# A fast attention, then an expert mixture: two more periods of short products in place of plain half layers

## The chip, the core and the metric
The kernel runs on one core of a Trainium2 chip: TensorE (matmuls; its weight loads are shown apart), VectorE (DVE), ScalarE (ACT), GpSimd (POOL), and SyncE (SP), which issues nearly all DMAs. The metric is the time of one execution in microseconds; before the change it is 1458.92 us, the median of 3 runs (1458.7 to 1458.94). The profile shows one execution.

## The reference
A gated linear attention over 4 batches, 8 heads, 768 steps of 48 wide heads, and behind it a dense mixture of 8 experts, with gates balanced by 8 rounds of row and column division:
```python
for t in range(S):
    state = f[:, :, t, :, None] * state + np.einsum('bhd,bhe->bhde', k[:, :, t], v[:, :, t])
    y[:, :, t] = einsum('bhd,bhde->bhe', q[:, :, t], state)
...
logits = x @ w_gate; P = exp(logits - logits.max())
for _ in range(8):
    P /= P.sum(1, keepdims=True) + 1e-09
    P /= P.sum(0, keepdims=True) + 1e-09
    P *= N / E
for e in range(E):                      # x: 3072 x 384, w1: 384 x 1024, w2: 1024 x 384
    out += P[:, e:e + 1] * (maximum(x @ w1[e], 0) @ w2[e])
```

## The kernel before
**Numbers.** Every product of 32-bit values is made of three 16-bit products (high by high, high by low, low by high). So each value is split: ScalarE writes the high part, VectorE or GpSimd the low part (the difference). `hh` and `hl` are the two parts of a hidden layer, `xh`/`xl` of the tokens, `sh`/`sl` of the attention's state.

**Attention.** 24 items of 128 tokens, each a chain of some 30 steps over all engines (`item`, L713): sigmoid of the gates, two scans (L732, L751), products (`aps`), the state (`st`, L814) and its parts (`sh` L821, `sl` L829), the output products (`yps`, the last eight of which read `sl`), the tokens' parts (L847, L850). A new item begins every 8 steps (STEPS), so three or four are under way. Each engine's order is fixed as the program is written (`pin`, `mm`): an engine that waits for one instruction holds up all behind it.

**Filler.** While the items run, TensorE works on experts 0 and 1 in the plain way. After each attention step `fill` (L955) takes as many units of this work as the table FILL says for that step; a unit is one matmul of 384 columns or three of 128. The work stands in `raw_pairs` (L941): for the first three half batches (u below TILED) it goes by tiles of 128 tokens (`moe_tile`, L444: a first layer `hps` in groups of four blocks, 36 matmuls of 128 columns each, ReLU into `hh` and `hl`, then a second layer `yps` of 384 columns, copied to `yr` and written to memory); for later ones by half batches of 384 tokens (`moe`, L400). A tile may only begin when its tokens are there. Then the gates are balanced, a chain of small steps between which LEAD units of the same filler are laid.

**Periods.** The rest goes by a scheme that makes block products of sums of blocks, with fewer products: ORDER (L96) lists the periods (expert, half of its hidden width, batch), 50 of them, each 15 slots: 90 matmuls of 256 columns for the first layer (banks `kb_A` to `kb_F`) and 126 of 192 columns for the second layer of the period before (`paired`, L1348: `kyps`, `kxps`). EVENTS says in which slot ScalarE, VectorE and GpSimd do what with the banks (`kr`, `kf`, `kgh`, `kgl`, `kal`); weights are prepared by `prepare_w1` and `prepare_w2` in the slots of W1AT, W2AT and their relatives. HALVED (L95) lists the batches of which expert 1's second half is made in periods at the end of ORDER; `plain` (L397) says how many of the 8 blocks of the hidden width the plain way does. It is used in `moe` alone. After the last period ENDING (L94) orders what is left: a '.' is one slot's events, a digit n takes block n two stages further.

Of the kernel before, what the change touches and what calls it, by code (L numbers as in the profile page):

```python
# [78 lines left out]
END = 27  # L79
W1AT = (0, 1, 2, 3, 5, 9, 10, 11, 12, 21, 23, 25, 26)  # L80
W1AT0 = (16, 18, 19, 19, 22, 23, 23, 27, 27, 33, 35, 40, 41)
W2AT = (4, 22, 25, 25, 27, 29, 30, 35, 38)
W2AT0 = (0, 1, 1, 3, 3, 5, 5, 5, 7)
W2AT1 = (3, 8, 10, 12, 13, 13, 14, 14, 19)
W2AT3 = (0, 3, 6, 13, 15, 18, 20, 21, 26)
READDAT = (9, 14)
CHECKAT = (1, 5)
# [3 lines left out]
ENDY = (None, None, 'B', 'D')  # L91
CONVAT = (3, 6, 7, 9, 11)
LAST_EVENTS = {18: (('gs', 'C', 1, 1), ('gs', 'C', 1, 2), ('hl', 'C', 1)), 19: (('gs', 'C', 1, 3), ('gf', 'F', 2), ('gh', 1, 0), ('gh', 1, 1))}
ENDING = '.0.1.01.1..12.1.22..23.23.34343444'  # L94
HALVED = (2, 3)  # L95
ORDER = [(e, m, b) for e in range(2, NE) for m in range(2) for b in range(B)] + [(1, 1, b) for b in HALVED]  # L96
PAIRED = (0, 1, 2)
BY_POOL = (1,)
# [9 lines left out]
TS = CT * C  # L108
ONES = CT * NP * D * 4
LEADS = 23  # L110
FILL = ((0, 11.7), (1, 10.3), (2, 0), (3, 0), (5, 2), (6, 0), (7, 6), (8, 6), (9, 0), (10, 6), (12, 5.3), (15, 5.3), (17, 5.3), (23, 8.7), (30, 8.7), (43, 8.0), (195, 7))
LEAD = 6.9
FIRSTAT = ((0,), (0,), (0, 4), (0, 7), (1, 9), (5, 10))
SECONDAT = ((16, 17), (18, 20), (17, 18), (17, 21), (20, 21), (20, 22), (24, 24), (24, 25))
# [169 lines left out]
def fast(ctx, tc, qkf, vbd, wg, w1, w2, out, flag):  # L284
# [37 lines left out]
    wctx, wctx0, wctx2, actx, pctx = (ExitStack() for _ in range(5))  # L322
    wp2 = wctx2.enter_context(tc.tile_pool(name="wp2", bufs=4, side="right"))
    wp1 = wctx.enter_context(tc.tile_pool(name="wp1", bufs=4, side="right"))
    wp0 = wctx0.enter_context(tc.tile_pool(name="wp0", bufs=8, side="right"))
    ap = actx.enter_context(tc.tile_pool(name="ap", bufs=2, side="right"))
    dp = ctx.enter_context(tc.tile_pool(name="dp", bufs=1, space=DRAM))
    psm = ctx.enter_context(tc.tile_pool(name="psm", bufs=2, space=PSUM))
# [113 lines left out]
    tiles, put_off, owed = [0], [False], []  # L442

    def moe_tile(e, u, t):  # L444
        w1s, w2s = ws[e]
        if (u, t) not in ready:
            raise RuntimeError("an expert is ahead of its tokens")
        xh, xl = xof(u)
        ts = slice(t * 128, t * 128 + 128)
        h = []  # L450
        for g in range(2):
            ps = bank([128, 4, 128], f"hps_{e}_{u}_{t}_{g}")
            n = 0
            for q, x in ((0, xh), (0, xl), (1, xh)):
                for f in range(4 * g, 4 * g + 4):
                    a = w1s[f // 2][q]
                    fs = slice((f % 2) * 128, (f % 2) * 128 + 128)
                    for k in range(KT):
                        mm(out=ps[:, f % 4, :], lhsT=a[:, k, fs], rhs=x[:, k, ts], start=(n == 0), stop=(q == 1 and k == KT - 1), skip_group_check=True)
                        n += 1  # L460
                        if n < 36:
                            yield 1 / 3
            i = tiles[0] % FT
            tiles[0] += 1
            th, tl = (hp.tile([128, 2, 256], F16, name=f"h{q}_{e}_{u}_{t}_{g}", tag=f"k{q}{i // 6}{i % 6 // 3}{i % 3}").rearrange("p c t -> p (c t)") for q in "hl")
# [12 lines left out]
        ps = bank([128, DM], f"yps_{e}_{u}_{t}")
        n = 0
        for f in range(FT):  # L480
            if len(owed) > 1 - f // 4:
                raise RuntimeError("a low part is owed")
            wh, wl = w2s[f // 2]
            hh, hl = (v[:, f % 4, :] for v in h[f // 4])
            for a, b in ((hh, wh), (hh, wl), (hl, wh)):
                mm(out=ps, lhsT=a, rhs=b[:, f % 2, :], start=(n == 0), stop=(n == 3 * FT - 1))
                n += 1
                if n < 3 * FT:
                    yield 1
# [449 lines left out]
    ws = [([None] * 4, [None] * 4) for e in range(NE)]  # L939

    def raw_pairs(pairs):  # L941
        for e in range(2):
            for t in range(TT):
                yield from moe_tile(e, 0, t)
        for u in range(1, TILED):
            for t in range(TT):
                for e in range(2):
                    yield from moe_tile(e, u, t)
        for e, u in pairs:
            if u >= TILED:  # L950
                yield from moe(e, u, ws[e])
# [138 lines left out]
        return (lambda: xq), lambda: sums(b), [x32[:, k].rearrange("p u t -> p (u t)") for k in range(KT)]  # L1090

    first = [load(0, 1 + n // 4, n % 4) for n in range(8)]
    second = [load(1, 1 + n // 4, n % 4) for n in range(8)]
    wgen = gate_weights()
    it = early_item(0)
    go(it)
# [22 lines left out]
    live, g = [it, nxt], 0  # L1119
    for n in range(2, 8):  # L1120
        at_steps(first[n], *FIRSTAT[n - 2])
    for n in range(8):
        at_steps(second[n], 4 + n, *SECONDAT[n])
    begin = {LEADS + STEPS * (i - 3): i for i in range(3, NT)}
    begin_tail = max(begin) + 17
# [339 lines left out]
    def at_all(n, slots, gen):  # L1465
        for slot in slots:
            at_slots(n + slot // PRODUCTS, (slot % PRODUCTS,), gen)

    for n, (e, m, b) in enumerate(ORDER):
        part = n % 4  # L1470
        if n - part + 4 < PERIODS and part in (0, 2):
            e2, m2, _ = ORDER[n - part + 4]
            gen = prepare_w1(e2, 2 * m2 + part // 2)
            at_all(n, W1AT if n else W1AT0, gen)
        if n == 0:
            at_all(0, W2AT0, prepare_w2(e, 2 * m))
            at_all(0, W2AT1, prepare_w2(e, 2 * m + 1))
        if n - part + 4 < PERIODS and (n in (1, 3) if n < 4 else part in (0, 2)):
            e2, m2, _ = ORDER[n - part + 4]
            at_all(n, W2AT if n != 3 else W2AT3, prepare_w2(e2, 2 * m2 + part // 2))  # L1480
        if n >= FIRST_READD:
            at_slots(n, READDAT, again)
        if n >= 5 and part in (1, 3):
            for s in CHECKAT:
                plan.setdefault((n, s), []).append(lambda: next(checks, None))
        if n >= 6 and part in (0, 2):
            at_slots(n, MAXAT, maxima)
        if n >= PERIODS - 2:
            at_slots(n, VERDICTAT[n - PERIODS], judged)
# [200 lines left out]
```

## Time and profile before
| | before |
|---|---|
| median of 3 runs | 1458.92 us |
| the profiled execution | 1458.97 us, its span 1457.2 us |
| TensorE busy | 1435.4 us (99%), 16188 matmuls |
| VectorE, ScalarE, GpSimd busy | 1241.6, 1112.2, 1092.3 us |
| attention items 3 to 23 (first to last mask product) | 78.6 to 346.3 us |
| the periods | from about 442 us |

Busy time of TensorE is modelled for its ends and its matmuls overlap; whether it is dense is read from the distance of the starts. Busy time of the others is measured.

### The profile page before, as it was taken

Reading aid. Unit: us, or ns where it says so; the run is one execution under the profiler, and the core shown is the slowest. Engines: PE = TensorE matmul, PEld = TensorE weight load, DVE = VectorE, ACT = ScalarE, POOL = GpSimd, SP = SyncE. Lnnn points to the kernel's source line nnn. Section 1 sums busy time; section 2 is a strip of 40 time slices with the busy share of each in tenths; the row PEclk is TensorE's granted clock in tenths of the full one; section 3 lists DMA queues with packets and bytes.
Section 4 is the critical chain, followed back from the end, with each engine's and each line's share of the span. In section 5 each row is a group of like instructions: output and inputs, shape, how many; then the busy total and the mean of one; then the engine's idle time right before and its main releaser. Section 6 shows DMA issues by size and latency. Waiting matters only on the chain.

```text
span 1457.2 us, 40795 instructions
## 1 busy us (share of the span) xinstructions
PE 1435.4 (99%) x16188; PEld 1267.0 (87%) x16188; DVE 1241.6 (85%) x2540; ACT 1112.2 (76%) x2492; POOL 1092.3 (75%) x1288
## 2 busy tenths in 40 slices
PE   7999999999999999999999999999999999999997
PEld 5788886666568899999999999999999999999997
DVE  8868878877868998888899898888888889888886
ACT  7767778875547778888888888888777787778874
POOL 3244665675625769999999999999888888888874
PEclk9999999999999999999999999999999999999999
DMA  9245544541111011222211111111000000000201
GB/s 265 84 113 132 120 110 126 124 120 47 65 49 35 24 40 47 56 62 61 61 55 58 49 50 45 41 51 49 23 23 24 23 23 23 13 15 20 77 13 69
DMA packets 82955, 90.54 MB, mean 62 GB/s; under 512 B 50017, under 2 KB 69601, under 8 KB 82754
## 3 DMA queue, kind: packets, MB, share of 16 engines
q1 hardware_dynamic: 82322, 87.25, 21.6%
q8 instruction: 128, 2.10, 0.6%
q14 instruction: 73, 0.60, 0.1%
q10 hardware_dynamic: 432, 0.59, 0.1%
HBM read 64.03 MB, written 14.16 MB: 54 GB/s over the span
## 4 chain that ended last, share of the span: by engine, by line
PE 73%; DVE 3%; ACT 1%; POOL 0%; issue 0%; ACTq 0%; POOLq 0%; DVEq 0%
PE kyps L312 29%; PE kb_A L312 9%; PE kb_B L312 8%; PE kb_D L312 6%; PE kxps L312 5%; PE kb_C L312 4%; PE yps L312 4%; PE hps L312 3%; PE kb_E L312 2%; PE kb_F L312 2%; DVE k1l L1228 0%; DVE kf L1538 0%; DVE kl L1569 0%; POOL k1s L1216 0%; DVE acc L1387 0%
## 5 line engine op out<-in xcount | busy, mean ns | idle before, releaser
L312 PEld LDWEIGHTS <-k1h 128*128 128x128 f16 x3000 | 282.5, 98 | 21.4 <-issue 1.1
L312 PE MATMUL kyps<-k2h,kgl 128*128 128x192 f16 x1188 | 292.3, 246 | 0.6 <-POOL kgl L1564 0.6
L312 PE MATMUL kyps<-k2h,kgh 128*128 128x192 f16 x1188 | 292.3, 246 | 0.1
L312 PE MATMUL kyps<-k2l,kgh 128*128 128x192 f16 x1188 | 292.2, 246 | 0.0
L312 PEld LDWEIGHTS <-kgh 128*128 128x128 f16 x2400 | 220.9, 98 | 7.2 <-issue 0.5
L1564 POOL TENSOR_TENSOR kgl<-kf,kgh 128x512 f16<-128x512 f32 x148 | 198.4, 1341 | 2.1 <-ACT kgh L1561 2.1
L1387 DVE SCALAR_TENSOR_TENSOR yy<-kyps,pes,part 128x192 f32<-128x192 f32 x270 | 111.5, 413 | 92.5 <-PE kyps L312 82.3
L1564 POOL TENSOR_TENSOR kgl<-kr,kgh 128x512 f16<-128x512 f32 x148 | 175.4, 1185 | 9.1 <-PE kyps L312 7.7
L1430 POOL TENSOR_TENSOR acc<-acc,yy 128x384 f32<-128x384 f32 x135 | 134.9, 1000 | 58.4 <-DVE yy L1387 58.4
L312 PEld LDWEIGHTS <-k1l 128*128 128x128 f16 x1500 | 146.8, 98 | 16.9
L312 PEld LDWEIGHTS <-kh 128*128 128x128 f16 x1200 | 112.6, 98 | 7.9 <-issue 1.3
L312 PEld LDWEIGHTS <-kgl 128*128 128x128 f16 x1200 | 117.4, 98 | 0.9 <-POOL kgl L1564 0.8
L312 PEld LDWEIGHTS <-w1h 128*128 128x128 f16 x1248 | 87.9, 98 | 27.1 <-issue 2.1
L312 PE MATMUL yps<-w2h,hl 128*128 128x384 f16 x336 | 110.1, 328 | 1.0 <-DVE hl L470 0.9
L312 PE MATMUL yps<-w2l,hh 128*128 128x384 f16 x336 | 110.0, 328 | 0.6 <-DVE w2l L385 0.6
L312 PE MATMUL yps<-w2h,hh 128*128 128x384 f16 x336 | 110.1, 328 | 0.2 <-ACT hh L420 0.2
L1515 ACT ACTIVATE cp<-kb_A 128x512 f32<-128x512 f32 x150 | 89.8, 599 | 17.5 <-DVE kb_A L1517 15.9
L1541 POOL TENSOR_TENSOR kr<-kr 128x256 f32<-128x256 f32 x100 | 75.6, 756 | 33.5 <-DVE xbl L1029 26.4
L312 PEld LDWEIGHTS <-hh 128*128 128x128 f16 x672 | 65.1, 99 | 37.2 <-issue 1.0
L1384 ACT ACTIVATE kyps<-kyps 128x192 f32<-128x192 f32 x148 | 47.7, 322 | 65.2 <-PE kyps L312 65.1
L1561 ACT ACTIVATE kgh<-kf 128x512 f16<-128x512 f32 x150 | 94.9, 633 | 1.7 <-DVE kf L1538 1.6
L1561 ACT ACTIVATE kgh<-kr 128x512 f16<-128x512 f32 x150 | 94.3, 629 | 0.6 <-DVE kr L1538 0.6
(323 smaller groups left out, 5383.6 us busy)
## 6 DMA issues: line engine op xcount, KB each, us to landing
q<-in_qkf_dram SPq DMA_DIRECT2D x23, 672.0 KB, 5.0
k1r<-in_w_dram SPq DMA_DIRECT2D x26, 384.0 KB, 3.0
k2r<-in_w_dram SPq DMA_DIRECT2D x26, 384.0 KB, 3.0
ys<-yr SPq DMA_DIRECT2D x48, 192.0 KB, 2.4
yb<-ys SPq DMA_DIRECT2D x48, 192.0 KB, 2.4
vr<-in_vbd_dram SPq DMA_DIRECT2D x24, 192.0 KB, 2.5
out_dram<-acc SPq DMA_DIRECT2D x21, 192.0 KB, 1.9
w1r<-in_w_dram SPq DMA_DIRECT2D x8, 384.0 KB, 9.4
```

The costliest lines, as they stand in the source:

```text
L312: ins = (nc.tensor.transpose if transpose else nc.tensor.matmul)(**kw)
L1384: pin(nc.scalar.activation(out=out, in_=in_, func=AF.Copy, **kw))
L1387: pin(nc.vector.scalar_tensor_tensor(out=y, in0=ps, scalar=p, in1=z, op0=ALU.mult, op1=ALU.add))
L1430: pin(nc.gpsimd.tensor_tensor(out=y, in0=y, in1=z.rearrange("p s d -> p (s d)"), op=ALU.add))
L1515: pin(nc.scalar.activation(out=fresh(ev[2]), in_=bk, func=AF.Copy))
L1541: pin((nc.gpsimd if ev[2] == 'P' else nc.vector).tensor_tensor(out=r[:, 0], in0=r[:, 1], in1=r[:, 0], op=ALU.subtract))
L1561: pin(nc.scalar.activation(out=hs['g', t][0][i], in_=hs['f' if i else 'r', t], func=AF.Copy))
L1564: pin((nc.vector if tag == str(PERIODS - 1) and ev[1] else nc.gpsimd).tensor_tensor(out=hs['g', t][1][i], in0=hs['f' if i else 'r', t], in ...
```

## The change
HALVED takes batches 0 and 1 too, so ORDER has 52 periods and expert 1 does half of its hidden width in the plain way for all tokens; `moe_tile` learns `plain`. Four loads of expert 1's weights go, and its pool holds four tiles. `moe_tile` yields 0 between its layers, and `raw_pairs` uses that to run the first layer of one tile ahead of the second layer of another. FILL gives fewer units for each step from 23 on (5.2 then 6.6, before 8.7 then 8.0). Two tables of preparation steps for the first periods and ENDING are different.
```diff
-W1AT0 = (16, 18, 19, 19, 22, 23, 23, 27, 27, 33, 35, 40, 41)
+W1AT0 = (16, 18, 19, 19, 22, 23, 23, 25, 26, 26, 29, 37, 40)
+W2ATB = (4, 12, 20, 20, 21, 22, 22, 35, 38)
-ENDING = '.0.1.01.1..12.1.22..23.23.34343444'
-HALVED = (2, 3)
+ENDING = '.0.1.01.11..2.1.22..23.23.34343444'
+HALVED = (0, 1, 2, 3)
-FILL = (... (17, 5.3), (23, 8.7), (30, 8.7), (43, 8.0), (195, 7))
+FILL = (... (17, 5.3), (23, 5.2), (43, 6.6), (107, 6.6), (195, 6.5))
-    wp0 = wctx0.enter_context(tc.tile_pool(name="wp0", bufs=8, side="right"))
+    wp0 = wctx0.enter_context(tc.tile_pool(name="wp0", bufs=4, side="right"))
...
-        for g in range(2):
+        fts = plain(e, u)
+        for g in range(fts // 4):
...
             yield 1 / 3
+        yield 0
         ps = bank([128, DM], f"yps_{e}_{u}_{t}")
         n = 0
-        for f in range(FT):
-            if len(owed) > 1 - f // 4:
+        for f in range(fts):
+            if len(owed) > fts // 4 - 1 - f // 4:
...
+        pending = []
+
+        def hidden(e, u, t):
+            gen = moe_tile(e, u, t)
+            for cost in gen:
+                if not cost:
+                    break
+                yield cost
+            pending.append(gen)
+
+        def rest(most):
+            while len(pending) > most:
+                yield from pending.pop(0)
+
         for e in range(2):
             for t in range(TT):
-                yield from moe_tile(e, 0, t)
+                yield from hidden(e, 0, t)
+                yield from rest(1 if plain(e, 0) < FT and t < TT - 1 else 0)
         for u in range(1, TILED):
             for t in range(TT):
                 for e in range(2):
-                    yield from moe_tile(e, u, t)
+                    yield from hidden(e, u, t)
+                    yield from rest(1 if e == 0 and plain(1, u) < FT else 0)
...
-    second = [load(1, 1 + n // 4, n % 4) for n in range(8)]
+    second = {n: load(1, 1 + n // 4, n % 4) for n in (0, 1, 4, 5)}
...
-            at_all(n, W2AT if n != 3 else W2AT3, prepare_w2(e2, 2 * m2 + part // 2))
+            at_all(n, {1: W2ATB, 3: W2AT3}.get(n, W2AT), prepare_w2(e2, 2 * m2 + part // 2))
```
The order on ScalarE in the attention, where the tile of expert 0 and then that of expert 1 go through (`hh_e_u_t_g` is group g of a tile's hidden layer, `yr_e_u_t` its result; `ft`, `tds`, `vhc`, `vh`, `xh`, `kb`, `vl`, `qh`, `ah`, `sh` belong to items). Before:
```order
L467 ACTIVATE hh_0_1_0_1_1885<-hps_0_1_0_1_1842 128x512
L725 ACTIVATE ft0_125<-q3_6_1778 112x8x63
L727 ACTIVATE tds_154<-q3_6_1778 112x8
L742 ACTIVATE vhc_6_1915<-vr_6_1780 128x384
L744 ACTIVATE vh0_136<-vr_6_1780 64x8x48 x2
L491 ACTIVATE yr_0_1_0_1990<-yps_0_1_0_1889 128x384
L847 ACTIVATE xh0_313<-yps_4_1928 96x3x128
L847 ACTIVATE xh0_313<-yps_4_1928 32x128 x3
L761 ACTIVATE kb0_124<-q3_6_1778 48x8x64 x2
L766 ACTIVATE vl0_140<-vlc_6_1916 64x8x48 x2
L467 ACTIVATE hh_1_1_0_0_2100<-hps_1_1_0_0_1993 128x512
```
The same place now:
```order
L745 ACTIVATE vhc_6_1733<-vr_6_1599 128x384
L747 ACTIVATE vh0_136<-vr_6_1599 64x8x48 x2
L469 ACTIVATE hh_1_1_0_0_1819<-hps_1_1_0_0_1717 128x512
L850 ACTIVATE xh0_313<-yps_4_1758 96x3x128
L850 ACTIVATE xh0_313<-yps_4_1758 32x128 x3
L764 ACTIVATE kb0_124<-q3_6_1597 48x8x64 x2
L769 ACTIVATE vl0_140<-vlc_6_1734 64x8x48 x2
L775 ACTIVATE qh_6_1896<-q3_6_1597 112x512
L494 ACTIVATE yr_0_1_0_1923<-yps_0_1_0_1823 128x384
L816 ACTIVATE ah_5_1928<-am_5_1912 128x512
L824 ACTIVATE sh1_146<-st_5_1807 48x8x48 x2
L494 ACTIVATE yr_1_1_0_1947<-yps_1_1_0_1926 128x384
```
Before, a tile's result `yr_0_1_0` stands ahead of the next tile's `hh_1_1_0_0`. Now expert 1's only group stands ahead of both results, and the pieces of the items stand closer to each other, with less filler between them.

The order on VectorE in the ending; blocks of period 48 (before) and 50 (now) are finished while the hidden layers of the last period, 49 and 51, are made. Before:
```order
L1569 SCALAR_TENSOR_TENSOR kl_49_1_26320<-kb_49_C_26529,kh_49_1_26319 128x512
L1538 SCALAR_TENSOR_TENSOR kf_49_1_26747<-kb_49_C_26529,kf_49_1_26747 128x256
L1550 SCALAR_TENSOR_TENSOR kal_49_2_26720<-kb_49_F_26590,kah_49_2_26719 128x256
L1387 SCALAR_TENSOR_TENSOR acc2_9129<-kxps_48_2_26696,pes_119,acc2_9129 128x192
L1387 SCALAR_TENSOR_TENSOR yy_48_2_26698<-kyps_48_2_26695,pes_119,part_48_2_26697 128x192
L1564 TENSOR_TENSOR kgl0_49_1_26761<-kr_49_1_26647,kgh0_49_1_26759 128x512
L1564 TENSOR_TENSOR kgl1_49_1_26762<-kf_49_1_26747,kgh1_49_1_26760 128x512
L1387 SCALAR_TENSOR_TENSOR acc2_9129<-kyps_48_2_26695,pes_119,acc2_9129 128x192
L1387 SCALAR_TENSOR_TENSOR yy_48_2_26698<-kyps_48_2_26695,pes_119,part_48_2_26697 128x192
```
The same place now:
```order
L1588 SCALAR_TENSOR_TENSOR kl_51_1_26423<-kb_51_C_26636,kh_51_1_26422 128x512
L1406 SCALAR_TENSOR_TENSOR acc2_8536<-kxps_50_2_26803,pes_119,acc2_8536 128x192
L1406 SCALAR_TENSOR_TENSOR yy_50_2_26805<-kyps_50_2_26802,pes_119,part_50_2_26804 128x192
L1557 SCALAR_TENSOR_TENSOR kf_51_1_26854<-kb_51_C_26636,kf_51_1_26854 128x256
L1569 SCALAR_TENSOR_TENSOR kal_51_2_26827<-kb_51_F_26697,kah_51_2_26826 128x256
L1583 TENSOR_TENSOR kgl0_51_1_26876<-kr_51_1_26754,kgh0_51_1_26874 128x512
L1583 TENSOR_TENSOR kgl1_51_1_26877<-kf_51_1_26854,kgh1_51_1_26875 128x512
L1406 SCALAR_TENSOR_TENSOR acc2_8536<-kyps_50_2_26802,pes_119,acc2_8536 128x192
L1406 SCALAR_TENSOR_TENSOR yy_50_2_26805<-kyps_50_2_26802,pes_119,part_50_2_26804 128x192
```
The additions into `acc2` and `yy` of the third block of the last period but one have gone ahead of the last `kf` and of `kal`.

## Rows read from the trace of the kernel before

**Rows 1.** the page, busy time of each engine in the whole execution
```profile
PE 1435.4 (99%) x16188; PEld 1267.0 (87%) x16188; DVE 1241.6 (85%) x2540; ACT 1112.2 (76%) x2492; POOL 1092.3 (75%) x1288
```

**Rows 2.** windows: length, busy us (instructions) PE, PEld, DVE, ACT, POOL, clock, DMA
```profile
36.70:78.60 41.90, 39.40 (x562) 31.32 (x561) 33.80 (x55) 31.79 (x61) 14.43 (x14) 1.00 0.33 90
78.60:346.30 267.70, 266.13 (x3901) 202.19 (x3899) 214.18 (x412) 201.96 (x435) 154.68 (x167) 1.00 0.47 116
228.30:281.00 52.70, 52.39 (x661) 36.02 (x659) 45.78 (x88) 42.45 (x92) 28.14 (x31) 1.00 0.52 126
...
442.00:500.00 58.00, 56.60 (x580) 51.86 (x579) 51.47 (x109) 45.83 (x105) 40.10 (x53) 1.00 0.09 29
600.00:1400.00 800.00, 799.86 (x8542) 759.24 (x8540) 706.21 (x1479) 645.36 (x1485) 711.80 (x830) 1.00 0.13 40
```

**Rows 3.** timeline of TensorE: start, length, engine, line, operation, count
```profile
119.81 0.33 PE L312 MATMUL yps<-w2l,hh 128*128 128x384 f16 x1
...
122.57 0.83 PE L312 MATMUL hps<-xh,w1h 128*128 128x128 f16 x12
123.24 0.83 PE L312 MATMUL hps<-xl,w1h 128*128 128x128 f16 x12
```

**Rows 4.** waits of TensorE from 33 us on: us in total, times, longest
```profile
PE kyps L312 <- DVE yy L1387: 1.2, 1, 1.2
PE yps L312 <- DVE hl L470: 0.9, 2, 0.7
PE kyps L312 <- POOL kgl L1564: 0.6, 1, 0.6
...
PE yps L312 <- DVE sl L829: 0.3, 1, 0.3
```

**Rows 5.** VectorE by shape, attention stretch: busy us, mean ns, idle before
```profile
L829 DVE SCALAR_TENSOR_TENSOR sl<-st,sh 48x384 f16<-48x384 f32 x34 | 29.0, 853 | 4.1 <-ACT sh L821 3.7
...
L421 DVE SCALAR_TENSOR_TENSOR hl<-hps,hh 128x384 f16<-128x384 f32 x36 | 19.7, 550 | 18.1 <-ACT hh L420 17.6
L470 DVE SCALAR_TENSOR_TENSOR hl<-hps,hh 128x512 f16<-128x512 f32 x27 | 18.4, 683 | 22.6 <-ACT hh L467 22.6
```

**Rows 6.** ScalarE, groups by shape in the attention stretch
```profile
L420 ACT ACTIVATE hh<-hps 128x384 f16<-128x384 f32 x36 | 17.5, 485 | 5.1 <-PE hps L312 4.6
...
L467 ACT ACTIVATE hh<-hps 128x512 f16<-128x512 f32 x26 | 15.5, 596 | 9.5 <-PE hps L312 9.2
...
L491 ACT ACTIVATE yr<-yps 128x384 f32<-128x384 f32 x14 | 6.8, 489 | 14.4 <-PE yps L312 9.0 <-issue 5.2 <-ACT sh L821 0.3
```

**Rows 7.** timeline of VectorE ahead of item 7's last products
```profile
137.85 0.69 DVE L470 SCALAR_TENSOR_TENSOR hl<-hps,hh 128x512 f16<-128x512 f32 x1 [1.05 <-ACT hh L467]
138.46 1.11 DVE L829 SCALAR_TENSOR_TENSOR sl<-st,sh 48x384 f16<-48x384 f32 x2
```

**Rows 8.** timeline of TensorE, matmuls that read sl in items 7 and 16
```profile
141.11 0.40 PE L312 MATMUL yps<-qh,sl 112*128 112x64 f16 x8
...
261.52 0.41 PE L312 MATMUL yps<-qh,sl 112*128 112x64 f16 x8 [0.31 <-DVE sl L829]
```

**Rows 9.** timeline of the ending, three engines around TensorE's wait
```profile
1438.46 0.41 DVE L1538 SCALAR_TENSOR_TENSOR kf<-kb_C,kf 128x256 f32<-128x256 f32 x1
...
1438.90 0.63 ACT L1561 ACTIVATE kgh<-kf 128x512 f16<-128x512 f32 x1 [0.63 <-DVE kf L1538]
...
1439.44 0.41 DVE L1387 SCALAR_TENSOR_TENSOR yy<-kyps,pes,part 128x192 f32<-128x192 f32 x1
...
1439.90 0.24 PE L312 MATMUL kyps<-k2h,kh 128*128 128x192 f16 x1 [1.16 <-DVE yy L1387]
```

**Rows 10.** timeline of item 5, GpSimd and VectorE side by side
```profile
109.61 1.16 POOL L822 TENSOR_TENSOR al<-am,ah 128x512 f16<-128x512 f32 x1 [2.08 <-ACT ah L813]
...
110.52 2.10 DVE L829 SCALAR_TENSOR_TENSOR sl<-st,sh 48x384 f16<-48x384 f32 x2 [0.65 <-ACT sh L821]
...
110.72 1.48 POOL L775 TENSOR_TENSOR ql<-q,qh 112x512 f16<-112x512 f32 x1
```

More of the change, by code (lines that the diff above doesn't have):

```diff
@@ L110 @@
 LEADS = 23
-FILL = ((0, 11.7), (1, 10.3), (2, 0), (3, 0), (5, 2), (6, 0), (7, 6), (8, 6), (9, 0), (10, 6), (12, 5.3), (15, 5.3), (17, 5.3), (23, 8.7), (30, 8.7), (43, 8.0), (195, 7))
+FILL = ((0, 11.7), (1, 10.3), (2, 0), (3, 0), (5, 2), (6, 0), (7, 6), (8, 6), (9, 0), (10, 6), (12, 5.3), (15, 5.3), (17, 5.3), (23, 5.2), (43, 6.6), (107, 6.6), (195, 6.5))
 LEAD = 6.9
@@ L485, in moe_tile @@
             for a, b in ((hh, wh), (hh, wl), (hl, wh)):
-                mm(out=ps, lhsT=a, rhs=b[:, f % 2, :], start=(n == 0), stop=(n == 3 * FT - 1))
+                mm(out=ps, lhsT=a, rhs=b[:, f % 2, :], start=(n == 0), stop=(n == 3 * fts - 1))
                 n += 1
-                if n < 3 * FT:
+                if n < 3 * fts:
                     yield 1
@@ L1121, in fast @@
         at_steps(first[n], *FIRSTAT[n - 2])
-    for n in range(8):
+    for n in second:
         at_steps(second[n], 4 + n, *SECONDAT[n])
```

## The prediction
> **What bounds the kernel now.** I read the page first: TensorE is busy for 99% of the span, VectorE for 85% [rows 1]. Busy there is not full speed, so I took the windows by stage next. In the attention stretch (78.6 to 346.3 us, items 3 to 23) TensorE is busy for 266.13 of 267.70 us, VectorE for 214.18 (80%), ScalarE for 201.96 (75%), GpSimd for 154.68 (58%); in the periods (600 to 1400 us) TensorE idles for 0.14 of 800 us [rows 2]. The timeline then says whether busy means dense. From 119.81 to 122.57 us lie 17 matmuls of 384 columns, one after the other: 162.4 ns each. Twelve of 128 columns take 0.67 us: 55.8 ns each [rows 3]. So TensorE sets the pace, and fewer matmuls mean less time as long as nobody makes it wait. The waits of TensorE come last: beyond the start they are few, 1.2 us for one addition in the ending, 0.9 us for low parts of the hidden layer, 0.6 for a low part made by GpSimd, 0.3 for the low part of the state [rows 4]. What the reader should keep from this: TensorE is the bound everywhere, but in the attention stretch VectorE and ScalarE are only 20 to 25% away from it.
>
> **What the matmuls give.** HALVED takes expert 1's second half for batches 0 and 1 out of the plain layers. By the order of instructions 324 matmuls of 128 columns go (nine tiles, 36 each), 36 first-layer and 144 second-layer matmuls of 384 columns: 324 x 55.8 ns + 180 x 162.4 ns = 18.1 + 29.2 = 47.3 us [rows 3]. Two periods come: 216 matmuls each, and 8542 matmuls in the 800 us of periods make 93.65 ns a matmul, 20.23 us a period [rows 2], 40.5 us for two. Net -6.85 us. All of what a period has on the other engines lies inside this 20.23 us, where they are hidden already; the two new ones use weights that are prepared anyway, so no preparation is added. Four weight loads with their conversions leave the start.
>
> **Where it is taken from.** By the order, between the first matmul of item 3 and that of item 23 there are 267 fewer matmuls of 128 columns, 116 fewer second-layer and 36 fewer first-layer ones: 14.9 + 18.8 + 5.8 = 39.5 us. Another 6.9 us lie before item 3, 0.8 behind item 23. So nearly all of it comes out of the stretch in which the other engines are fullest; the attention work itself stays. Were TensorE dense throughout, the stretch would last 267.7 - 39.5 = 228.2 us.
>
> VectorE sheds only the low parts of the dropped hidden tiles there: 7 of 683 ns and 4 of 550 ns [rows 5], 7.0 us, so it needs 207.2 of 228.2 us: 91%, from 80%. ScalarE sheds 7 x 596 + 4 x 485 ns and gains one copy of a result (about 485 ns, as the same engine takes for the same width) [rows 6]: 196.3 us, 86%. GpSimd sheds nothing: 68%.
>
> Does TensorE wait for that? The tightest handoff is the low part of the state, sl, which the last eight matmuls of an item read. In item 7 sl ends at 138.46 + 1.11 = 139.57 us and TensorE comes to it at 141.11: 1.54 us spare; in item 16 nothing is spare and TensorE waits 0.31 us [rows 7, 8]. The 21 items read in this way lie between these two or a little above (to 3.2 us), the middle one at 1.8. Six attention steps lie between an item's first products and these matmuls, and each loses 1.4 units (8.0 to 6.6) of 162.4 ns: 1.36 us in all. If sl were made just as long after those products as now, the spare time of a middle item shrinks to 0.4 us, and the four tightest items (spare 0.06 to 1.25) lose 1.3, 0.5, 0.3 and 0.1 us: 2.2 us. Against that, VectorE stands idle before hl because it waits for ScalarE, 22.6 + 17.6 us in the stretch [rows 5], and 1.05 us of it before sl in item 7 [rows 7]; a faster TensorE lets these waits shrink. For it, the load of 91% with hardly a lull. I take 3.0 us of new waits, near the count by items; the lower end is -0.3 (the present sl wait gone as well), the upper end is under the rivals.
>
> **The order of tiles.** In the first tiled token tiles the second layer of expert 0 now stands behind the first layer of expert 1. That gives the low part hl the time of 36 matmuls of 128 columns (2.0 us) before it is read, where TensorE waited 0.9 us in two places [rows 4]. ScalarE and VectorE have the same instructions. The gain is at most 0.9. In the other direction the steps 23 to 42 lose 3.5 units each, 0.57 us a step, which brings items 3 and 4 closer to what they need; from 36.7 to 78.6 us TensorE loses 6.9 of 41.9 us and VectorE, busy for 33.80 [rows 2], loses two low parts and four weight conversions, some 5 us, so its share stays near 81%. I let these cancel: 0, with -0.9 and +3 as ends.
>
> **The period tables.** W1AT0 and W2ATB issue preparation steps of the first periods up to ten slots earlier, on SP, ScalarE, VectorE and GpSimd. TensorE idles for 1.40 us from 442 to 500 us [rows 2], 0.6 of it for GpSimd's kgl [rows 4]. The steps could clear that or double it: 0, with -1.4 and +1.4 as ends.
>
> **The ending.** TensorE's order there is unchanged. On VectorE two additions (acc, yy) go ahead of kf and kal. TensorE stands 1.16 us until yy, which starts at 1439.44; kf starts at 1438.46, three places earlier, so a place is worth 0.33 us and yy comes 0.65 us earlier [rows 9]. Behind kf, which is now two places late, waits ScalarE's kgh [rows 9], and behind that its copies for the next block; this takes back some of it. -0.5, between -0.65 and +0.3.
>
> **The sum.** -6.85 + 3.0 + 0 + 0 - 0.5 = -4.35. The profiled execution took 1458.97 us (span 1457.2 and 1.8 around it), 0.05 above the median of the runs: 1454.6 us.
>
> **The rivals.**
> 1. Everything arrives. Spare time holds because VectorE's idle time before hl is what goes. For it: VectorE runs nearly without a pause where it is late and TensorE is not held up (0.3 us in 21 items). Against: item 16, and three more with 1.3 us or less to spare. -6.85 - 0.65 - 0.9 = -8.4: 1450.6 us.
> 2. No change. TensorE waits a third of a microsecond for sl or hl in each of the 21 items, 7.0 us in place of 3.0: 1458.6 us. For it: the order in which VectorE works is fixed, so each late result delays what is queued behind it.
> 3. VectorE becomes the bound of the attention stretch, and it is slower. From 228.3 to 281.0 us, the fullest stretch of this length, it is busy for 45.78 of 52.70 us, 87% [rows 2]; if in-order waits between it, ScalarE and GpSimd allow no more over the whole stretch, its 207.2 us last 238.2, 10.0 more than TensorE needs: -6.85 - 0.5 + 10.0 = +2.65. Collisions with GpSimd add: in item 5 GpSimd's al and ql run from 109.61 to 112.20 us, and the two sl instructions beside them take 2.10 us [rows 10], where a pair alone takes 1.11 [rows 7]. 34 long ones average 853 ns against 555: 10 us in the stretch [rows 5]. With GpSimd at 68% instead of 58% that becomes 11.7, VectorE's need 208.9, and its stretch 240.1: the time would be 1458.97 - 7.35 + 11.9 = 1463.5 us. It decides from 207.2 / (228.2 + 7.35) = 88%: below this share of VectorE the change loses. Against: that 87% was seen while TensorE set the pace, and part of the rest was waiting for TensorE's own products.
>
> On these collisions the Trainium skill ("SBUF — State Buffer", Who interferes with whom) says that a VectorE instruction with two SBUF inputs and a GpSimd instruction that reads SBUF exclude each other for their whole length. The trace agrees: the second sl of that item runs to just behind the end of ql. By the rule each meeting costs whole instructions, so rival 3 deserves more than the mean load alone would give it.
>
> **How the numbers follow.** Chances: forecast 0.42 (own range 1452.4 to 1457.0), rival 1 0.25, rival 2 0.15, rival 3 0.18. About 0.2%, 2.9 us, is what a measurement of this kernel tells from no change: faster is below 1456.0, slower above 1461.8. Faster: rival 1 and four fifths of the forecast's case, 0.59. Same: the rest of that, rival 2 and some of rival 3 (its price without collisions is 1461.6), 0.25. Slower: 0.16. The range reaches from rival 1's middle, with a gain of the period tables, 1450.0, to most of rival 3, 1462.5.
>
> **What will show it.** The windows of the stretch between items 3 and 23: about 231 us if I am right, 228 for rival 1, 238 or more for rival 3, with VectorE at 90% of it, over 91% or 87%. In the waits of TensorE sl, and hl of the plain tiles, must be the new names, 2 to 4 us. The ending's wait for yy should read about 0.5 us. A period must still take 20.2 us. I am wrong if TensorE idles in the stretch for more than 5 us, or if new waits stand in the first periods or before item 3.

## The result, and the profile after

| kernel | median, us | runs | profiled execution (span) |
|---|---|---|---|
| before | 1458.94 | 5 | 1458.97 (1457.2) |
| changed | 1475.21 (1473.79 to 1476.85) | 5 | 1476.85 (1475.0) |

The ratio is 1.0111, 95% interval 1.0099 to 1.0122: 16.3 us slower, where I had forecast 4.3 us faster. The profiled execution is the slowest of the five, 1.6 us above their median; the sums below are made in it. Its granted TensorE clock over the whole span is 0.991, that of the other four 0.993 (each rounded to a thousandth). So those lost some 3 us less to the low clock that is described below (0.002 of 1475 us).

The page's line of engines answers to [rows 1]. TensorE's share falls from 99% to 97%: it stands still 38 us instead of 22.

```profile
PE 1436.6 (97%) x16116; PEld 1275.5 (86%) x16116; DVE 1264.7 (86%) x2587; ACT 1129.4 (77%) x2541; POOL 1119.9 (76%) x1314
```

The windows by stage answer to [rows 2] (length, busy us and instructions of TensorE, weight loads, VectorE, ScalarE, GpSimd, then the granted clock). Items 3 to 23 now run from 74.9 to 320.9 us.

```profile
36.70:74.90 38.20, 32.88 (x467) 25.96 (x465) 28.37 (x48) 26.33 (x53) 10.05 (x12) 0.96 0.29 81
74.90:320.90 246.00, 232.20 (x3481) 176.48 (x3479) 214.85 (x401) 195.35 (x427) 161.75 (x170) 0.98 0.52 127
74.90:100.00 25.10, 21.25 (x333) 18.20 (x331) 18.08 (x36) 16.54 (x37) 13.76 (x14) 0.86 0.60 125
150.00:250.00 100.00, 96.07 (x1390) 70.68 (x1389) 92.67 (x172) 83.12 (x182) 70.26 (x76) 1.00 0.54 134
...
442.00:500.00 58.00, 54.95 (x569) 51.56 (x567) 47.48 (x104) 41.76 (x97) 35.21 (x46) 0.97 0.08 23
600.00:1400.00 800.00, 799.94 (x8546) 759.49 (x8544) 705.19 (x1474) 645.06 (x1480) 708.36 (x824) 1.00 0.12 36
```

A period is what it was: 8546 matmuls in 800 us, 20.22 us for 216. The attention stretch lasts 246.0 us where 228.2 would be dense and I had expected 231. Two columns tell how: TensorE stands 13.8 us, and its clock is 0.98 there, 0.86 between 74.9 and 100 us. VectorE's share of the stretch is 87.3%, but unevenly: 72% up to 100 us, and 93% in the 100 us from 150 us on.

TensorE's waits from 33 us on, answering to [rows 4] (us in total, times, longest):

```profile
PE yps L313 <- DVE sl L832: 4.6, 7, 1.2
PE kvb L313 <- DVE kvb L795: 3.9, 1, 3.9
PE yps L313 <- DVE hl L422: 3.2, 2, 2.4
PE yps L313 <- DVE hl L472: 3.0, 1, 3.0
PE kyps L313 <- POOL kgl L1583: 2.9, 1, 2.9
PE lps L313 <- DVE am L810: 2.2, 3, 1.3
...
PE kyps L313 <- DVE yy L1406: 0.5, 1, 0.5
PE kyps L313 <- ACT part L1403: 0.4, 1, 0.4
```

Four of them are the long ones: hl at 61 us, kvb at 82 us, hl at 281 us (2.4 of the 3.2), kgl at 451 us. `kvb` is the bank of an item's products of k and v, which VectorE first clears with two memsets; `am` are an item's masked products. The timeline shows what stands ahead of the first two on VectorE (start, length, engine, line, operation).

```profile
58.71 1.22 DVE L735 TENSOR_TENSOR_SCAN r<-ft,ind 112x512 f32<-112x512 f32 x1
...
60.29 0.64 DVE L750 SCALAR_TENSOR_TENSOR q<-q,r 112x512 f32<-112x512 f32 x1
60.50 0.33 PE L313 MATMUL yps<-w2h,hl 128*128 128x384 f16 x1
60.85 0.55 DVE L751 SCALAR_TENSOR_TENSOR vlc<-vr,vhc 128x384 f16<-128x384 f32 x1
61.32 1.22 DVE L754 TENSOR_TENSOR_SCAN q<-ft,pi 112x512 f32<-112x512 f32 x1
62.57 1.46 DVE L756 TENSOR_TENSOR q<-q 112x512 f32<-112x512 f32 x1
63.95 0.68 DVE L472 SCALAR_TENSOR_TENSOR hl<-hps,hh 128x512 f16<-128x512 f32 x1
64.69 0.34 PE L313 MATMUL yps<-w2h,hl 128*128 128x384 f16 x1 [3.05 <-DVE hl L472]
...
83.60 1.21 DVE L754 TENSOR_TENSOR_SCAN q<-ft,pib 112x512 f32<-112x512 f32 x1
84.73 1.43 DVE L853 SCALAR_TENSOR_TENSOR xl<-yps,xh 96x384 f16<-96x384 f32 x4
86.18 0.17 DVE L794 MEMSET kvb<- 112x128 int32 x1
86.42 0.07 DVE L795 MEMSET kvb<- 112x8 int32 x1
86.63 0.24 PE L313 MATMUL kvb<-vhc,kt 128*128 128x48 f16 x2 [3.85 <-DVE kvb L795]
...
88.18 0.52 PE L313 MATMUL yps<-w2h,hh 128*128 128x384 f16 x1
88.50 0.52 PE L313 MATMUL yps<-w2l,hh 128*128 128x384 f16 x1
```

VectorE does not pause: hl, itself 0.68 us, stands behind an attention item's five instructions, and the memsets, 0.24 us together, behind a scan and four low parts. The last two rows show something else. Matmuls of 384 columns now start 0.32 us apart, where they start 0.16 apart at 60.8 us, ahead of the first wait. Windows on the stretches behind the four long waits (the clock is the third column from the end):

```profile
65.00:69.00 4.00, 4.00 (x29) 2.81 (x27) 0.42 (x1) 1.46 (x5) 1.67 (x3) 0.57 0.52 122
86.60:93.00 6.40, 6.37 (x69) 5.53 (x70) 1.33 (x3) 1.64 (x3) 3.57 (x4) 0.53 0.49 54
284.00:288.00 4.00, 4.00 (x57) 3.17 (x58) 3.01 (x8) 2.17 (x4) 3.07 (x3) 0.60 0.22 76
454.50:458.00 3.50, 3.50 (x21) 3.03 (x22) 0.51 (x2) 2.47 (x6) 3.42 (x5) 0.52 0.08 15
```

Behind each TensorE is granted 1.2 GHz for some microseconds. Length times missing clock is 1.7 + 3.0 + 1.6 + 1.7 = 8.0 us. VectorE, busy for 1.33 of 6.40 us in the second, now waits for the slowed TensorE: it does not use the time to catch up (e14 below shows this).

**The sum by stages.** Counting, for each stage, the time between starts of matmuls beyond what their columns take at 2.4 GHz, the changed kernel has more than before by 4.15 us ahead of item 3, 17.8 in the attention stretch (some 6 of them by 100 us), 0.4 in the balance, 2.7 from 442 to 500 us, and 0.3 less behind that: 24.8 us. The matmuls themselves are 6.86 us less. 24.8 - 6.9 = 17.9, and the two profiled executions differ by 1476.85 - 1458.97 = 17.9 us.

### The profile page after: what moved, and what is told of

Its sections match the earlier page's. It is cut to its first block, busy times and chain, and to the rows that moved or that the text cites. A ratio compares the mean times of both kernels' runs of the same rounds, so it can differ in the third digit from the quotient of the medians.

```text
span 1475.0 us, 40791 instructions
## 1 busy us (share of the span) xinstructions
PE 1436.6 (97%) x16116; PEld 1275.5 (86%) x16116; DVE 1264.7 (86%) x2587; ACT 1129.4 (77%) x2541; POOL 1119.9 (76%) x1314
## 4 chain that ended last, share of the span: by engine, by line
PE 82%; DVE 10%; ACT 4%; issue 2%; POOL 1%; DMA 0%; ACTq 0%; POOLq 0%; DVEq 0%
PE kyps L313 30%; PE kb_B L313 9%; PE kb_A L313 9%; PE kb_D L313 7%; PE yps L313 6%; PE kxps L313 5%; PE kb_C L313 5%; PE hps L313 5%; PE kb_E L313 2%; PE kb_F L313 2%; DVE sl L832 1%; DVE r L735 1%; DVE hl L422 1%; DVE xl L853 1%; DVE q L754 1%
## 5 line engine op out<-in xcount | busy, mean ns | idle before, releaser
L313 PEld LDWEIGHTS <-k1h 128*128 128x128 f16 x3120 | 294.0, 98 | 21.0 <-issue 0.5
L313 PE MATMUL kyps<-k2h,kgl 128*128 128x192 f16 x1236 | 304.4, 246 | 2.9 <-POOL kgl L1583 2.9
L313 PE MATMUL kyps<-k2h,kgh 128*128 128x192 f16 x1236 | 304.3, 246 | 0.5 <-ACT part L1403 0.4
L313 PE MATMUL kyps<-k2l,kgh 128*128 128x192 f16 x1236 | 304.3, 246 | 0.0
L313 PEld LDWEIGHTS <-kgh 128*128 128x128 f16 x2496 | 230.0, 98 | 8.0 <-issue 1.0
L313 PE MATMUL yps<-w2h,hl 128*128 128x384 f16 x288 | 95.1, 330 | 6.2 <-DVE hl L422 3.2
L313 PE MATMUL yps<-w2l,hh 128*128 128x384 f16 x288 | 95.1, 330 | 1.1 <-DVE w2l L386 1.1
L313 PEld LDWEIGHTS <-w1h 128*128 128x128 f16 x1008 | 74.5, 100 | 24.8 <-issue 2.7
L313 PE MATMUL yps<-w2h,hh 128*128 128x384 f16 x288 | 95.0, 330 | 0.0
L1403 ACT ACTIVATE kxps<-kyps 128x192 f32<-128x192 f32 x156 | 49.4, 317 | 53.9 <-PE kyps L313 47.7
```

The costliest lines, as they stand in the source:

```text
L1403: pin(nc.scalar.activation(out=out, in_=in_, func=AF.Copy, **kw))
```

## The experiments

Theory from here on: in a step of the attention TensorE has only FILL units beside the item's own products; this cover is the time in which VectorE's in-order queue gets its results ready. The change takes it away in two places, 23 to 42 and from 43 on. Rivals: the order of tiles, the added periods, or GpSimd and ScalarE. The kernel before was timed again beside every batch of runs (medians 1458.87 to 1459.19 us). The changed kernel was timed once, so what is said against it below are differences of medians; the range of its five runs overlaps none of the runs compared with it.

| run | median, us | against before, 95% interval |
|---|---|---|
| e1 straight tiles | 1486.16 | 1.0174 to 1.0202 |
| e2 old tables | 1472.22 | 1.0072 to 1.0099 |
| e3 before, less cover | 1473.59 | 1.0085 to 1.0116 |
| e4 three halves | 1463.57 | 1.0018 to 1.0040 |
| e5 kvb early | 1470.45 | 1.0070 to 1.0097 |
| e6 before, early cover | 1472.59 | 1.0077 to 1.0108 |
| e7 less VectorE | 1468.52 | 1.0049 to 1.0077 |
| e8, e11, e12 three halves, other cover | 1465.64, 1467.49, 1464.06 | 1.0022 to 1.0071 over all three |
| e9 before, new order | 1457.93 | 0.9983 to 1.0001 |
| e10 before, new ending | 1459.03 | 0.9990 to 1.0008 |
| e13 kvb and tables | 1468.43 | 1.0050 to 1.0077 |
| e14 clock cover | 1471.95 | 1.0076 to 1.0107 |
| e15 order and ending | 1457.72 | 0.9983 to 1.0001 |
| e16 e15 and kvb early | 1456.80 | 0.9978 to 0.9996 |

**e3 and e6, less cover in the kernel before.** One table, no matmul added or dropped.

```diff
-FILL = (..., (23, 8.7), (30, 8.7), (43, 8.0), (195, 7))
+FILL = (..., (23, 8.7), (30, 8.7), (43, 6.6), (160, 8.0), (195, 7))   # e3
+FILL = (..., (23, 5.2), (43, 8.5), (195, 7))                          # e6
```

> The kernel before with one table changed: FILL 6.6 in place of 8.0 for the steps 43 to 159 of the attention; the same matmuls, 117 x 1.4 x 162.4 ns = 26.6 us of them moved behind the attention, where TensorE is dense. Theory (the cover per step is what keeps TensorE from waiting for VectorE; 1.4 units a step less cost 6 to 12 us between items 5 and 20): 1464 to 1470 us, with new waits for sl and hl. Rival (VectorE has the slack that the prediction gave it, 2 to 3 us of waits): 1461 to 1462 us. Second rival (cover is no matter, the order of tiles and batch 0 make the waits): 1459 us.

> The kernel before with FILL alone changed: 5.2 units in place of 8.7 in steps 23 to 42 (as the changed kernel has it), 8.5 in place of 8.0 from step 43; the same matmuls in all, 20 x 3.5 = 70 units moved behind step 42. Theory (the lack of cover in these steps, by whatever cause, makes TensorE wait for kvb and hl there): 5 to 9 us of waits between 57 and 100 us, 1463 to 1468 us. Rival (the loss there needs the halved tiles and their order): 1459 to 1460 us.

Both lose more than expected, 14.5 and 13.5 us. In e3 the waits are those of the changed kernel, spread over items 5 to 23 and the balance (`sk_c` are the balance's matmuls):

```profile
PE yps L312 <- DVE sl L829: 3.3, 3, 1.7
PE yps L312 <- DVE hl L470: 2.9, 7, 0.7
PE sk_c L312 <- DVE sk_cs L1188: 2.2, 2, 1.9
PE hps L312 <- DVE hl L421: 2.1, 1, 2.1
...
PE lps L312 <- DVE am L807: 1.4, 1, 1.4
```

In e6 the two long ones stand at the places of the changed kernel, with 1.2 GHz behind each (one of 2.2 us in the balance comes to them):

```profile
PE kvb L312 <- DVE kvb L792: 4.5, 1, 4.5
PE yps L312 <- DVE hl L470: 4.2, 2, 4.1
```

So neither the halved tiles nor the order nor the periods are needed to make these losses; FILL alone does. In e3 VectorE is busy for 240.65 of the 291.40 us from 78.6 to 370 us, 83% on average: the share alone would not have shown the loss.

**e1, the tiles in their old order.**

```diff
-                yield from hidden(e, 0, t)
-                yield from rest(1 if plain(e, 0) < FT and t < TT - 1 else 0)
+                yield from moe_tile(e, 0, t)
...
-                    yield from hidden(e, u, t)
-                    yield from rest(1 if e == 0 and plain(1, u) < FT else 0)
+                    yield from moe_tile(e, u, t)
```

> The changed kernel with one part undone: each tile's second layer again stands right behind its own first layer (the order of the kernel before); 52 periods, FILL and tables as changed. Theory (too little cover: in steps 23 to 42 the dropped work of batch 0 leaves only 5.2 units a step, and TensorE arrives before VectorE): the wait for kvb (3.9 us) and the waits for sl, hl and am in the attention stay, at most the 3.0 us wait for hl at 61 us goes with its 1.2 GHz stretch: 1470 to 1476 us. Rival (the order of tiles put hl behind an attention item's work on VectorE, and that is the main cause): 10 us or more go, 1465 us or less.

Neither: 11 us slower still. Each second layer again follows its own first layer at once, and with few units a step TensorE waits for the high parts, 7.5 us between 100 and 360 us:

```profile
PE yps L313 <- ACT hh L469: 7.5, 6, 2.2
PE yps L313 <- DVE hl L422: 3.2, 2, 2.4
PE yps L313 <- DVE sl L831: 2.7, 4, 1.2
```

The order of tiles is the part of the change that helps. The hl wait at 61 us stays without it (3.0 us), so the order did not make it.

**e9, the order alone in the kernel before** (the functions hidden and rest as above, applied to all tiled units).

> The kernel before with the order of tiles alone changed (a token tile's second layer of expert 0 behind the first layer of expert 1, for all three tiled units); 50 periods, FILL and tables as before. Theory (the order gives hl more time and costs nothing as long as the cover stays; without it the changed kernel lost 11 us more): within 2 us of the kernel before, 1457 to 1460 us. Rival (the order puts low parts behind an item's work on VectorE and costs by itself): 1462 us or more.

1.3 us faster by the medians, the interval just reaching over 1: the 0.9 us of hl waits [rows 4] are gone, kvb waits 0.7 in place of 0.3.

**e4, three halved batches.**

```diff
-HALVED = (0, 1, 2, 3)
+HALVED = (1, 2, 3)
-second = {n: ... for n in (0, 1, 4, 5)}
+second = {n: ... for n in range(8)}
-FILL = (..., (23, 5.2), (43, 6.6), (107, 6.6), (195, 6.5))
+FILL = (..., (23, 8.7), (30, 8.7), (43, 7.3), (195, 7))
...
```

> The changed kernel with HALVED (1, 2, 3): 51 periods, batch 0's second half of expert 1 stays in the plain layers with its four weight loads, FILL 8.7 in steps 23 to 42 as before and 7.3 from 43, tables of the first periods as before. Net matmul work -3.4 us. Theory (the loss from 57 to 100 us comes from batch 0's work taken out of steps 23 to 42): that stretch is back at the length it had before (0 to 1 us of waits), the attention behind it loses 1 to 4 us at 7.3 units: 1455 to 1460 us. Rival (the order of tiles, which batch 1 still has, or the added periods): 1465 us or more.

The stretch up to 100 us is as before, so batch 0's work was what lacked there. By my count of the units it cannot be filled from elsewhere (with 5.8 units a step the plain layers reach unit 1 before its tokens, which come from item 3, exist); no run shows this. But 4.6 us remain, with 3.4 us less matmul work: hl at 241 us (2.3 us, and 1.7 of clock) and sk_c in the balance (4.0 us).

**e8, e11, e12, cover moved to those places.**

```diff
-FILL = (..., (43, 7.3), (195, 7))
+FILL = (..., (43, 7.0), (115, 7.8), (160, 7.5), (195, 7))   # e8, with LEAD 8.2
+FILL = (..., (43, 7.3), (112, 8.0), (136, 7.1), (195, 7))   # e11, with LEAD 7.3
+FILL = (..., (43, 7.3), (112, 8.0), (136, 7.1), (195, 7))   # e12, LEAD 6.9, HASTE (3, "PAV", 24, 60, 1, 1)
```

HASTE says at which step of the balance the sums of a batch's tokens start.

> Three halved batches as in e4, with other cover: FILL 7.0 in steps 43 to 114, 7.8 in 115 to 159, 7.5 from 160 (where VectorE has the sums of batches 0 and 1 beside the attention), and LEAD 8.2 in place of 6.9 (cover per step of the balance, whose matmuls sk_c waited 4.0 us for VectorE in e4). Theory (cover where VectorE is fullest is all it takes): the wait for hl at 241 us with its 1.2 GHz stretch (4.1 us) and most of the 4.0 us for sk_c go, 1 us comes between items 5 and 14: 1455 to 1458 us, a little faster than the kernel before. Rival (moving cover only moves the waits): 1461 to 1464 us.

> Three halved batches as in e4, FILL 7.3 from step 43, 8.0 in steps 112 to 135, 7.1 from 136, and LEAD 7.3 in place of 6.9. Theory (the wait for hl at 241 us and its 1.2 GHz stretch were worth 4.1 us, the waits for sk_c 4.0 us; a little more cover at both places takes the first and half of the second, and leaves enough plain work for the balance): 1457 to 1460 us. Rival (cover taken from elsewhere opens waits of the same length there): 1463 us or more.

> As e11 with LEAD 6.9, and the sums of batch 3's tokens start at step 24 of the balance instead of 12 (HASTE), so that VectorE has less beside the balance. Theory: sk_c waits below 2 us in place of 4.0, hl at 241 us gone, 1457 to 1460 us. Rival (the sums land in the first periods, where VectorE is nearly full too): 1463 us or more, with new waits between 420 and 500 us.

All three miss. The wait at 241 us is gone in each, and others came: in e8 the balance ends after its cover, and the periods wait for its result (`pes`, the gates).

```profile
PE sk_c L313 <- DVE sk_cs L1207: 2.7, 2, 2.3
PE kb_touchk L313 <- DVE pes L1212: 2.4, 1, 2.4
PE yps L313 <- DVE hl L422: 2.0, 2, 1.6
```

In e11 and e12 TensorE waits 3.5 and 2.9 us for hl at 347 us. Cover given to one place was missing at the next.

**e7, less work for VectorE.** Items 4 to 23 use the low part of V of item 3, so part of the attention is not computed.

```diff
-        pin(nc.vector.scalar_tensor_tensor(out=vlc, in0=vr, ...))
+        if i == 3:
+            pin(nc.vector.scalar_tensor_tensor(out=vlc, in0=vr, ...))
```

> The changed kernel, in which items 4 to 23 leave out the low part of V (vlc, one VectorE instruction of 0.55 us each; they use that of item 3): 20 x 0.55 = 11 us less on VectorE, all other engines as they are. Theory (VectorE's in-order queue is what TensorE waits for in the attention): the waits for kvb, sl, hl and am shrink by 4 to 8 us with the clock, 1467 to 1471 us. Rival (the waits come from the chain of an item through GpSimd, ScalarE and the DMA): 1474 to 1476 us.

By the medians 6.7 us faster for 11 us less on VectorE alone: sl 4.6 to 3.2 us, am 2.2 to 0.3, hl 3.2 to 2.4 (L422), kvb 3.9 to 3.5. The two profiled executions, both with a clock of 0.991, differ by 5.0 us. So these waits come from VectorE's queue; no run takes work from GpSimd or ScalarE alone.

**e5, the memsets early, and e14, TensorE kept running.**

```diff
         yield from wait(3)
+        if i >= MERGED and 'kv' not in held_banks:        # e5, moved up from behind aps
+            held_banks['kv'] = ...; memset(words, 0); memset(words[:, ::C // 4], 1)
...
+        if i == MERGED:                                   # e14 alone
+            warm(18)
```

> The changed kernel with the two memsets of kvb five places earlier in VectorE's queue: ahead of q, vlc, the scan q and the low parts xl of item 3, that is some 4 us earlier. Theory (TensorE stands 3.9 us at the first kvb product because a 0.2 us memset is queued in order behind 4 us of an item's work, and the clock falls behind that wait): the wait falls to below 1 us, the 1.2 GHz stretch from 86 to 92 us (3.1 us) goes, and some of it comes back at the products that need am; 1469 to 1473 us. Rival (VectorE as a whole is late there, the memset's place is no matter): the same wait stands one product later, 1475 us.

> The changed kernel with 18 idle matmuls of 512 columns (18 x 213 ns = 3.8 us, their result is not read) in front of the first kvb products: TensorE runs through the 3.9 us in which it waited for the memset, nothing arrives earlier. Theory (the clock falls because TensorE stood for some 4 us, and the slow stretch behind is a cost of its own): no 1.2 GHz from 86 to 92 us, 2 to 3 us faster, 1472 to 1473 us. Rival (the clock falls for another reason, or the slow stretch only fills time in which VectorE is late anyway): 1475 us or more.

e5: 4.8 us faster; the wait is 0.4 us, 0.6 us came back at xl. e14 makes nothing arrive earlier, and is 3.3 us faster; windows of it on the wait and on the stretch behind it have the clock at 1.00, where it was 0.53:

```profile
82.00:86.00 4.00, 3.95 (x40) 1.94 (x38) 3.82 (x10) 2.30 (x4) 2.32 (x2) 1.00 0.61 204
86.00:93.00 7.00, 7.00 (x132) 6.67 (x128) 3.99 (x7) 5.54 (x12) 4.27 (x5) 1.00 0.49 115
```

So the slow stretch is a cost of its own beside the wait. Its price can be read by setting the two traces side by side: VectorE's memset comes 1.2 us earlier than in the changed kernel (85.21 in place of 86.42 us), its sl at 105 us 4.0 us earlier (101.33 in place of 105.29), and it stays at 4.0 us until 280 us. That makes 2.7 us for the stretch at kvb. The 1.3 us gained ahead of it and 1.4 us near 285 us are not the idle matmuls' doing: the waits for hl there are as long as before (3.1 and 2.4 us), but in this execution no low clock follows them. Each of the three is a little less than its length times missing clock (1.7, 3.0 and 1.6). The waits for sl, hl and am are as long as in the changed kernel, so VectorE had indeed gained nothing from the slow stretch. The granted clock of e14's four runs is 0.994 to 0.995, of the changed kernel's five 0.991 to 0.993.

**e2, the old tables, and e13, with e5's memsets.**

```diff
-W1AT0 = (16, 18, 19, 19, 22, 23, 23, 25, 26, 26, 29, 37, 40)
+W1AT0 = (16, 18, 19, 19, 22, 23, 23, 27, 27, 33, 35, 40, 41)
-            at_all(n, {1: W2ATB, 3: W2AT3}.get(n, W2AT), ...)
+            at_all(n, {3: W2AT3}.get(n, W2AT), ...)
```

> The changed kernel with the tables of the first periods as they were before (W1AT0, and W2AT in place of W2ATB). Theory (the three stages lose independently; the tables cost the 2.9 us wait for kgl at 451 us and the 1.2 GHz stretch behind it, some 1.5 us): 4 to 4.5 us less, about 1471 us, and TensorE's wait for kgl back at 0.6 us. Rival (the wait comes from the two added periods or from the later state of the preparation, not from the tables): it stays, 1475 us.

> The changed kernel with both single repairs: the kvb memsets early (e5, 4.8 us faster than the changed kernel) and the old tables of the first periods (e2, 3.0 us). Theory (the losses of the stages are separate waits, so they add): 1475.2 - 4.8 - 3.0 = 1467.4, within 1.5 us; what is left is the hl wait at 61 us and the attention's 10 us. Rival (a removed wait is paid again further on): 1470 us or more.

e2 is 3.0 us faster, and no 1.2 GHz follows 451 us. In the changed kernel GpSimd's timeline shows the step that W2ATB put ahead of kgl:

```profile
451.36 1.14 POOL L1265 TENSOR_TENSOR k2s<-k2r 128x192 f32<-128x192 f32 x2 [8.49 <-PE kyps L313]
452.46 0.46 POOL L1235 TENSOR_TENSOR k1s<-k1s,k1r 128x128 f32<-128x128 f32 x1
452.87 0.46 POOL L1235 TENSOR_TENSOR k1s<-k1r,k1s 128x128 f32<-128x128 f32 x1
453.28 1.16 POOL L1583 TENSOR_TENSOR kgl<-kr,kgh 128x512 f16<-128x512 f32 x1
```

GpSimd stands 8.5 us at k2s, which TensorE's kyps released, and three preparation steps are then done before kgl. The two tables were not undone one by one. e13 comes within 1.0 us of the sum of both repairs: the losses are separate.

**e10, the ending alone, and e15 and e16, the best.**

```diff
-ENDING = '.0.1.01.1..12.1.22..23.23.34343444'
+ENDING = '.0.1.01.11..2.1.22..23.23.34343444'
```

> The kernel before with ENDING alone changed. The prediction's step: the 1.16 us wait for yy falls to about 0.5 us, 0.5 us faster, 1458.5 us. By the changed kernel's trace a new wait of 0.4 us for part takes some of it back: 0.3 us faster, 1458.7 us. Rival (VectorE's places don't matter there): 1459.0 us.

> The version to which the runs point: the kernel before with two parts of the change, the order of tiles (e9, 1.2 us faster) and the ending (e10, 0.1 us); 50 periods, FILL and tables as before. Theory: 1457.8 us. Rival (e9's gain was within its uncertainty): 1459 us.

> As e15, with the kvb memsets early as in e5. In e9 TensorE waits 0.7 us for them. Theory: 0.5 us faster than e15, 1457.3 us. Rival (with the old cover the next wait takes its place): 1457.8 us.

e10 cannot be told from before, though its trace has the wait for yy at 0.5 us and the new one for part at 0.4. e15 is e9 with e10. e16, with the memsets early as well, is faster than both kernels: 1456.80 us, ratio 0.9987 (0.9978 to 0.9996). Its first row of waits is 1.4 us for kb at the start; kvb is gone from the list.

## Why the prediction was wrong

In the terms of the prediction's sum, beside the matmuls: some 10 us in place of 0 up to 100 us, 12 in place of 3.0 in the rest of the attention (10.0 of waits, 1.6 of low clock), 0.4 in the balance, 2.7 in place of 0 at the tables, and -0.3 in place of -0.5 behind them. The three signs of being wrong that the prediction named all came: TensorE idle for 13.8 us in the stretch, a longer wait in the first periods (kgl, 2.9 us in place of 0.6), and one ahead of item 3 (hl at 61 us).

- **"-6.85" of matmuls: right.** The columns dropped are worth 6.86 us in the trace, a period 20.22 us.
- **"I let these cancel: 0", steps 23 to 42: the first step that failed.** I weighed 0.57 us a step against VectorE's share (81%) and put +3 as the end. It cost some 10 us: 3.0 and 3.9 us of waits and 4.7 of low clock, less 1.2 us that TensorE waits there in before. A share says nothing of a queue. The timeline of before has the two engines meet at kvb within 0.3 us:

```profile
91.13 0.07 DVE L792 MEMSET kvb<- 112x8 int32 x1
91.25 0.21 PE L312 MATMUL kvb<-vhc,kt 128*128 128x48 f16 x2 [0.33 <-DVE kvb L792]
```

With 3.5 units a step less TensorE was there at 82.8 us and VectorE, its queue unbroken, at 86.5. I had read this stretch by its share alone; [rows 4] leave this wait of 0.3 us out.
- **"I take 3.0 us of new waits" in the attention: mis-sized.** They are 10.0 us (sl 4.6, hl 3.2, am 2.2), of which kvb is not a part. I let each item start with the old spare time. But VectorE works in order and takes what it is late into the next item, and the hl and am I did not count wait in the same queue. I also had its need shrink to 207.2 us; it is 214.85. The low parts sl, 34 long ones, average 1023 ns against 853 [rows 5], 5.8 us more:

```profile
L832 DVE SCALAR_TENSOR_TENSOR sl<-st,sh 48x384 f16<-48x384 f32 x34 | 34.8, 1023 | 7.5 <-ACT sh L824 7.1
```

- Of these 34, those that overlap no GpSimd instruction average 548 ns in before (14 of them) and 550 ns now (6), all between 537 and 556; the others 1066 ns (20) and 1124 ns (28). So most of the growth is that more of them meet GpSimd, which is busy for 66% of the stretch in place of 58%. The Trainium skill ("SBUF — State Buffer", Who interferes with whom), on which the prediction leaned for rival 3, says that a VectorE instruction with two SBUF inputs contends with a GpSimd instruction that reads SBUF. The two traces agree with it in kind.
- **Rival 3 had the right engine**, at a chance of 0.18, and the length of the stretch nearly right, in part by luck: 238.2 to 240.1 us, where it is 241.4 without the 4.6 us of low clock in it. Its price takes 87% as the most that VectorE can do, from the fullest piece of before. That piece was not the fullest: the same length from 245.0 us on has 90%.

```profile
245.00:297.70 52.70, 52.39 (x651) 35.87 (x650) 47.60 (x92) 42.06 (x94) 30.27 (x34) 1.00 0.49 120
```

And the changed kernel has 93% for 100 us. That its mean is 87% again is the average of such unequal pieces. I was right that VectorE can do more than 87%, and wrong to take comfort in it: TensorE waited for the order of VectorE's queue, in e3 at a mean share of 83%.

- **The tables, "0, with -1.4 and +1.4": outside.** 2.7 us in the trace, 3.0 by e2. I named GpSimd's kgl as the place, but not that a step put earlier can wait for TensorE and hold up the queue.
- **The clock had no term.** 8.0 us of the 24.8 are TensorE at 1.2 GHz behind four waits (some 3 us less in the other four runs, by their granted clock). In before it is 1.00 in every window from 36.7 us on [rows 2]; I had waits of a microsecond in mind and did not ask what a longer one brings.
- **The order of tiles, "at most 0.9": about right for the kernel before**, 1.3 us by e9, whose interval reaches over 1. But taken out of the changed kernel it costs 11 us (e1): with less cover the order is worth far more, and the sum had no term for that.
- **The ending, "-0.5": right in kind**, 0.5 us of wait as forecast; with the new 0.4 for part some 0.3 is left, and e10 sees 0.2, within its uncertainty.

Open: why the low clock follows one wait and not another like it (below); what GpSimd and ScalarE alone would give back; and whether some distribution of cover makes 51 periods pay; the four tried do not.

## What to carry to other kernels

Work on the bounding engine can be cover for another engine's queue. Before taking it out, move the same amount elsewhere in the old kernel and time that: e3 and e6 show the loss without any of the change. The share of a second engine gives no limit: here VectorE reached 93% over 100 us, and TensorE waited for it at a mean of 83% (e3). Follow its in-order queue up to every handoff, not only the tightest. Price a wait of some microseconds on TensorE at 1.4 to 1.8 times its length, as those here cost with the low clock behind them, until a trace shows the clock behind it.

## What the runs showed of the hardware

- Behind waits of 1.9 to 4.5 us TensorE was mostly granted 1.2 GHz, though it was busy again at once: in the changed kernel for some 3 to 6 us (twice the missing clock of the four windows). Eighteen idle matmuls in the place of one such wait kept it at 2.4 GHz; the stretch had cost 2.7 us.
- Not always: over the eighteen traces, 25 of the 35 waits of 1.8 us or more, from 36 us on, had low clock behind them. The shortest of them is 1.9 us long (e7, at 277 us), the longest without it 3.5 us (e11, at 347 us). In the changed kernel low clock follows the 3.0 us wait for hl at 61 us, in e5 the same wait, also at 61 us, has none behind it (windows of e5):

```profile
65.00:69.00 4.00, 4.00 (x62) 3.48 (x61) 1.46 (x3) 2.52 (x7) 1.78 (x3) 1.00 0.75 176
```

The five runs of the changed kernel lie 3.1 us apart, those of before 0.5. Stretches that are there in one run and not in another would do that, and the granted clock of the slowest, 0.991 in place of 0.993, says that it has some 3 us more of them; where they lie in the other runs is not known.
